# A weight remainder moved from TensorE to VectorE, and a chunk's state update joined with its outputs

## The chip, the cores and the metric

One core of a Trainium2 chip runs the whole program; the other cores are not used. The metric is the time of one execution on the device in microseconds (us). In the rows of the profile PE is TensorE's matmuls, PEld its weight loads, DVE VectorE, ACT ScalarE, POOL GpSimd, and SP SyncE, which issues most of the transfers.

## The reference

A gated linear attention over 768 steps for 4 x 8 heads of size 48, followed by two MLP layers on 3072 tokens of width 384 with 2048 hidden units.

```python
for t in range(S):                         # S = 768, state D x D = 48 x 48 per head, complex
    ar, ai = (a_re_n[:, :, t, :, None], a_im_n[:, :, t, :, None])
    new_re = ar * S_re - ai * S_im
    new_im = ar * S_im + ai * S_re
    kv = np.einsum('bhd,bhe->bhde', k[:, :, t], v[:, :, t])
    S_re, S_im = (new_re + kv, new_im)
    y[:, :, t] = np.einsum('bhd,bhde->bhe', q[:, :, t], S_re)
...
h = x @ w_in                               # first MLP: 384 -> 2048
g = h * np.tanh(softplus(h))
x = g @ w_out                              # 2048 -> 384
...
h = x @ w_in2                              # second MLP
g = h * np.clip(h + 3.0, 0.0, 6.0) / 6.0
out = g @ w_out2
```

Here a_re_n and a_im_n are the decay, scaled to a magnitude under one.

## The kernel before

**Blocks and chunks.** Tokens are worked in 12 blocks of 256 (three for each batch entry); a block is two chunks of 128 steps. For each block `elementwise` (VectorE and ScalarE, lines 589 to 682) forms running products of the decay and multiplies them into q and k. `spread` (L713, twelve transfers issued by SyncE) then lays the results out by head as `rq` and `rk`, and these must be read before the next block's `elementwise` may write `tq` (its first VectorE instruction is L591, behind ScalarE's L590).

**A chunk on TensorE.** `chunk` transposes k (`pk`, evicted by ScalarE as `kt`) and forms the scores (`psc`, L739), which VectorE masks (`am`, L741). `advance` multiplies `kt` with v to the state's update (`pu`, L756), and VectorE carries it into the state `sT`. `second` forms the outputs: `py<-am` (L785) from the masked scores and, except in a sequence's first chunk, `py<-rq,sd` (L791) from the state at the chunk's start, which `turn` transposes (`pst`) and ScalarE evicts as `sd`. The matmuls of `pu` and `py` write 64 rows each; in the profile one such block of eight f32 products is 16 instructions. `pk`, `psc`, `pst`, `pu` and `py` share two PSUM buffers.

**The MLP layers.** Weights and activations are held as two f16 parts, a rounded one (hi) and the remainder (lo), and each product is three matmuls (hi hi, hi lo, lo hi) of 128x256: `ph` (L889) for 384 to 2048, `oa` and `oB` (L902) for 2048 to 384. Between them stand ScalarE's activation, a VectorE multiplication (`s`, L912 or L919), ScalarE's rounding to `gh` (L925) and VectorE's remainder `gl` (L926). `ph` has three PSUM buffers. The layers run as (first MLP, block 0), (first, 1), (second, 0), (first, 2), (second, 1) and so on.

**Weights.** The two weight sets (w1i, w1o for the first MLP, w2i, w2o for the second) come from HBM as 64-bit floats, in 24 pieces of 512 columns for each set. `weights` takes a piece apart: ScalarE converts the low words (L840), VectorE joins the words to an f32 (L841, L842), ScalarE rounds it to the hi part (L843). TensorE then forms the remainder: an f32 matmul of the value with a scaled identity `small` (L845) and an f16 one of the hi part with a negative identity `minus` (L846) add up in a buffer `pw`, which has the tag of `ph`, and ScalarE evicts it as the lo part (L847). The first set is made before the first layer; the second set's pieces are handed out while the first two layers run. Its staging tile `wst` has two buffers and its f32 tile `wt` one.

**The order of the work.** The program is written in one order, and then `arrange` gives each engine another: `survey` lists the instructions with their dependencies and a cost for each, and `plan` schedules them by list, with the costs, in three rounds, and keeps the best. The engines run in exactly that order. Matmuls of 64 rows that `survey` puts into one of its `runs` are scheduled as one piece that stands together; each new run is charged 250 ns more.

Of the kernel before, what the change touches and what calls it, by code (L numbers as in the profile page):

```python
# [10 lines left out]
F32 = mybir.dt.float32  # L11
# [3 lines left out]
AF = mybir.ActivationFunctionType  # L15
ALU = mybir.AluOpType
# [34 lines left out]
SWO = 2.0 ** 5  # L51
# [192 lines left out]
def survey(instructions, first, labels):  # L244
    ENG = mybir.EngineType
    tensor, vector, scalar, pool, sync = ENG.PE, ENG.DVE, ENG.Activation, ENG.Pool, ENG.SP
    after = (tensor, vector, scalar, pool)
    bufs = {"ph": PHB, "oa": 2, "pa": 2, "am": 2, "s1": SPB, "gh": LAG + 1, "gl": LAG + 1, "x2_hi": X2B, "x2_lo": X2B, "wst": 2, "td": 2}
    size = lambda ap: math.prod(n for _, n in ap[1:])

    def adjacent(ap):
        run = 1
        for step, count in list(ap.ap)[:0:-1]:
            if step != run and count > 1:
                break
            run *= count
        return run

    ops, label, tags = [], [], [x[1] for x in labels]
    marks = [x[0] for x in labels] + [1 << 60]  # L260
    j = 0
    for k in range(first, len(instructions)):
        i = instructions[k]
        while marks[j + 1] <= k:
            j += 1
        if i.engine in after or "DMA" in type(i).__name__:
            ops.append(i)
            label.append(tags[j])
    n = len(ops)
    preds = [dict() for _ in range(n)]  # L270
    runs, where, stage = [], {}, {}
    seen, users, rows = {}, {}, {}
    cost, issue, dma, port = [0.0] * n, [0.0] * n, [False] * n, [False] * n
    for k, i in enumerate(ops):
        aps = [(x, False) for x in i.ins if hasattr(x, "bass_ap")] + [(x, True) for x in i.outs if hasattr(x, "bass_ap")]
        tiles = [(x.bass_ap, mybir.dt.size(x.dtype), wr) for x, wr in aps]
        out = tiles[-1][0]
        for ap, width, wr in tiles:
            name = ap.tensor.name
            tag = getattr(ap.tensor, "tag", None)  # L280
            if tag is None:
                continue
            key = tag.split("_")[0] if not tag.startswith("x2_") else tag[:5]
            wr = wr or key in ("oa", "oB")
            whole = key in ("ph", "oa", "oB", "pa", "td")
            box = (0, 128, 0, 1 << 30)
            if not whole:
                p0, lo = divmod(ap.offset, ap.ap[0][0])
                lo += sum(s * (c - 1) for s, c in ap.ap[1:] if s < 0)
                hi = lo + sum(abs(s) * (c - 1) for s, c in ap.ap[1:]) + 1  # L290
                box = (p0, p0 + ap.ap[0][1], lo * width, hi * width)
            if name not in seen:
                seen[name], users[name] = [], []
                row = rows.setdefault(tag, [])
                if row:
                    preds[k][users[row[-1]][0]] = ops[users[row[-1]][0]].engine != i.engine
                row.append(name)
                old = len(row) - 1 - bufs.get(key, 1)
                if old >= 0:
                    for p in users[row[old]]:  # L300
                        preds[k][p] = True
            if users[name]:
                first_use = users[name][0]
                if first_use != k:
                    preds[k].setdefault(first_use, ops[first_use].engine != i.engine)
            users[name].append(k)
            keep = []
            for b, p, pw in seen[name]:
                if (wr or pw) and b[0] < box[1] and box[0] < b[1] and b[2] < box[3] and box[2] < b[3] and p != k:
                    preds[k][p] = preds[k].get(p, False) or pw or ops[p].engine != i.engine  # L310
                if wr and p != k and box[0] <= b[0] and b[1] <= box[1] and box[2] <= b[2] and b[3] <= box[3]:
                    continue
                if not wr and not pw and b == box and tag.startswith("w"):
                    continue
                keep.append((b, p, pw))
            keep.append((box, k, wr))
            seen[name] = keep
        free = max(size(ap.ap) for ap, _, _ in tiles)
        if "DMA" in type(i).__name__:
            dma[k] = True  # L320
            count = math.prod(c for _, c in out.ap)
            issue[k] = 450.0 if out.ap[0][1] > 32 else 625.0
            cost[k] = count * tiles[-1][1] / (360.0 if min(adjacent(ap) * w for ap, w, _ in tiles) >= 2048 else 175.0)
        elif i.engine == tensor:
            passes = 1 if tiles[0][1] == 2 else 2 if i.is_transpose else 4
            cost[k] = passes * size(out.ap) / 2.4 + (2.0 if passes == 1 else 8.0)
            if out.ap[0][1] == 64:
                cost[k] = 115.0
                last = runs[-1][-1] if runs else -1
                if runs and label[last] == label[k] and out.tensor.name == where[last] and stage[last] == tiles[0][0].tensor.tag.split("_")[0]:  # L330
                    runs[-1].append(k)
                else:
                    runs.append([k])
                    cost[k] += 250.0
                where[k], stage[k] = out.tensor.name, tiles[0][0].tensor.tag.split("_")[0]
        elif i.engine == vector:
            fast = type(i).__name__ == "InstMemset" or (type(i).__name__ == "InstTensorScalarPtr" and len(tiles) == 2)
            steps = max(abs(ap.ap[-1][0]) * w for ap, w, _ in tiles)
            cost[k] = 66.0 + free / (1.92 if fast else 0.96) * (1.5 if steps >= 32 else 1.0)
            sb = [ap for ap, _, wr in tiles if not wr and getattr(ap.tensor, "tag", "").split("_")[0] not in ("ph", "oa", "oB", "pa")]  # L340
            port[k] = len(sb) >= 2 or fast
        elif i.engine == scalar:
            psum = tiles[0][0].tensor.tag.split("_")[0] in ("ph", "oa", "oB", "pa")
            cost[k] = (51.0 if psum else 94.0) + 93.0 * sum(size(ap.ap) == 1 for ap, _, _ in tiles) + free / 1.2
        else:
            cost[k] = 46.0 + free * 2.083
            port[k] = True

    return ops, label, preds, cost, issue, dma, port, runs
# [128 lines left out]
def fast_path(ctx, tc, a, out, flag):  # L478
    nc = tc.nc
    mm = nc.tensor.matmul  # L480
    act = nc.scalar.activation
    tt = nc.vector.tensor_tensor
    ts = nc.vector.tensor_scalar
    stt = nc.vector.scalar_tensor_tensor
# [12 lines left out]
    ps_h = ctx.enter_context(tc.tile_pool(name="ps_h", bufs=PHB, space=PSUM))  # L497
# [7 lines left out]
            name=nc.get_next_instruction_name(),  # L505
# [42 lines left out]
    minus = const.tile([128, 2, 128], F16, name="minus")  # L548
    small = const.tile([128, 128], F32, name="small")
# [278 lines left out]
    def weights(idx, nm, s, o):  # L828
        if idx < 2:
            j = next(stage)  # L830
            st = spare(j % 10).bitcast(I32).rearrange("p (n t) -> p n t", t=2)
            t = spare(10 + j % 4 // 2)[:, j % 2 * 1024:][:, :1024].bitcast(I32)
        else:
            st = stp.tile([128, 512, 2], I32, name="wst")
            t = wt.tile([128, 512], I32, name="wt")
        nc.sync.dma_start(out=st, in_=a[nm].bitcast(I32)[:, 2 * o:2 * (o + 512)].rearrange("p (n t) -> p n t", t=2))
        hw, lw = st[:, :, 1], st[:, :, 0]
        tf = t.bitcast(F32)
        hi, lo = W[nm][0][:, o:o + 512], W[nm][1][:, o:o + 512]
        act(out=lw, in_=lw.bitcast(U32), func=AF.Copy, scale=LOW3, bias=-0.5)  # L840
        stt(t, hw, 3, lw, op0=ALU.logical_shift_left, op1=ALU.bitwise_or)  # L841
        stt(t, hw, BUT_SIGN, t, op0=ALU.bitwise_or, op1=ALU.bitwise_and)  # L842
        act(out=hi, in_=tf, func=AF.Copy, scale=s * 2.0 ** -128)  # L843
        pw = ps_h.tile([128, 512], F32, name="pw", tag="ph")
        mm(pw, small, tf, start=True, stop=False)  # L845
        mm(pw, minus[:, idx % 2], hi, start=False, stop=True)  # L846
        act(out=lo, in_=pw, func=AF.Copy, scale=s / SWO)  # L847
        yield

    def weight_guard():  # L850
# [11 lines left out]
    stage = iter(range(24))  # L862
# [116 lines left out]
    start = len(nc.cur_bb.bb.instructions)  # L979
# [133 lines left out]
```

## Time and profile before

| | |
|---|---|
| three executions | 1038.88, 1039.21, 1034.57 us (median 1038.88) |
| the profiled execution | 1037.71 us, span 1035.8 us |
| TensorE busy | 968.7 us, 94% of the span, 8719 matmul instructions |
| VectorE busy | 800.5 us, 77% |
| ScalarE busy | 675.2 us, 65% |
| mean granted clock of TensorE | 0.983 of full speed |

The span runs from the first to the last instruction of the program; the profiled execution's own time has 1.9 us around it. The busy time of an engine is the union of its instructions' times. An instruction's recorded time overlaps with the next one's on TensorE and VectorE, so what one costs in a dense row is read from start to start.

### The profile page before, as it was taken

How to read it: one execution, taken by the hardware profiler on the slowest of the kernel's cores; microseconds unless marked ns; L12 is line 12 of the kernel's file. 1: busy time of each engine (PE TensorE's matmuls, PEld its weight loads, DVE VectorE, ACT ScalarE, POOL GpSimd, SP SyncE). 2: the span in 40 equal slices, each digit the busy share in tenths (PEclk: the TensorE clock that was granted, in tenths of full speed). 3: DMA queues.
4: the chain of work that ended last, by engine and by line, in shares of the span. 5: the costliest groups of instructions: out<-in, count | busy, mean ns of one | idle time of the engine just before them, and what ended most of it. 6: DMA issues, size and time to landing. Idle time of an engine off the chain costs nothing.

```text
span 1035.8 us, 21145 instructions
## 1 busy us (share of the span) xinstructions
PE 968.7 (94%) x8719; PEld 817.9 (79%) x8719; DVE 800.5 (77%) x1455; ACT 675.2 (65%) x1181; POOL 0.9 (0%) x7
## 2 busy tenths in 40 slices
PE   3576889999999999999999999999999999999998
PEld 1144577788888888887888888888887988988887
DVE  7978779979699695895797996895994996654532
ACT  7865789955856846846747747747647747637532
POOL 0000000000000000000000000000000000000000
PEclk9888999999999999999999999999999999999999
DMA  9771854550615126029027146327237227222000
GB/s 357 287 137 45 157 169 143 135 106 24 119 37 100 43 68 112 1 68 166 3 91 158 53 114 151 98 89 156 84 108 131 83 85 155 85 69 77 22 16 19
DMA packets 58681, 106.64 MB, mean 103 GB/s; under 512 B 6482, under 2 KB 40018, under 8 KB 58578
## 3 DMA queue, kind: packets, MB, share of 16 engines
q1 hardware_dynamic: 53586, 100.50, 39.0%
q10 hardware_dynamic: 4992, 4.72, 1.4%
q8 instruction: 70, 1.15, 0.5%
q14 instruction: 33, 0.27, 0.1%
HBM read 80.35 MB, written 4.79 MB: 82 GB/s over the span
## 4 chain that ended last, share of the span: by engine, by line
PE 60%; DVE 16%; ACT 10%; DMA 9%; SPq 2%; issue 2%; ACTq 0%; DVEq 0%
PE ph L889 25%; PE oa L902 16%; PE oB L902 8%; DMA rk<-tq 5%; PE psc L739 3%; PE pw L845 2%; SPq L713 2%; PE py L785 1%; DMA rq<-inp 1%; DVE gl L926 1%; DMA yr<-yr 1%; PE py L791 1%; ACT s L909 1%; DVE s L919 1%; DVE tq L682 1%
## 5 line engine op out<-in xcount | busy, mean ns | idle before, releaser
L926 DVE TENSOR_TENSOR gl<-s,gh 128x512 f16<-128x512 f32 x192 | 131.9, 687 | 53.4 <-ACT gh L925 52.8
L925 ACT ACTIVATE gh<-s 128x512 f16<-128x512 f32 x192 | 120.1, 625 | 76.0 <-DVE s L919 64.2
L889 PE MATMUL ph<-x_hi,w1i_hi 128*128 128x256 f16 x576 | 158.4, 276 | 6.3 <-ACT x_hi L817 3.7
L889 PE MATMUL ph<-x_lo,w1i_hi 128*128 128x256 f16 x576 | 158.6, 276 | 0.2 <-DVE x_lo L818 0.2
L889 PE MATMUL ph<-x_hi,w1i_lo 128*128 128x256 f16 x576 | 158.3, 275 | 0.0
L889 PE MATMUL ph<-x_hi,w2i_hi 128*128 128x256 f16 x576 | 157.1, 273 | 0.0
L889 PE MATMUL ph<-x_hi,w2i_lo 128*128 128x256 f16 x576 | 157.1, 273 | 0.0
L889 PE MATMUL ph<-x_lo,w2i_hi 128*128 128x256 f16 x576 | 157.1, 273 | 0.0
L889 PEld LDWEIGHTS <-w1i_hi 128*128 128x128 f16 x1152 | 113.9, 99 | 23.8 <-issue 8.5
L902 PEld LDWEIGHTS <-w1o_hi 128*128 128x128 f16 x1152 | 113.2, 98 | 20.6 <-issue 6.2
L902 PEld LDWEIGHTS <-w2o_hi 128*128 128x128 f16 x1152 | 112.2, 98 | 16.2 <-issue 4.0
L889 PEld LDWEIGHTS <-w2i_hi 128*128 128x128 f16 x1152 | 111.9, 98 | 14.7 <-issue 2.7
L918 ACT ACTIVATE s<-ph,half 128x512 f32<-128x512 f32 x96 | 65.5, 682 | 80.7 <-PE ph L889 80.6
L902 PE MATMUL oa<-gl,w1o_hi 128*128 128x256 f16 x384 | 105.1, 274 | 4.2 <-DVE gl L926 4.0
L902 PE MATMUL oa<-gh,w1o_hi 128*128 128x256 f16 x384 | 105.2, 274 | 3.2 <-ACT gh L925 3.2
L902 PE MATMUL oa<-gl,w2o_hi 128*128 128x256 f16 x384 | 104.7, 273 | 0.7 <-DVE gl L926 0.7
L902 PE MATMUL oa<-gh,w1o_lo 128*128 128x256 f16 x384 | 105.0, 273 | 0.0
L902 PE MATMUL oa<-gh,w2o_hi 128*128 128x256 f16 x384 | 104.7, 273 | 0.0
L902 PE MATMUL oa<-gh,w2o_lo 128*128 128x256 f16 x384 | 104.7, 273 | 0.0
L919 DVE SCALAR_TENSOR_TENSOR s<-s,ph 128x512 f32<-128x512 f32 x96 | 65.5, 682 | 43.1 <-ACT s L918 42.8
L912 DVE SCALAR_TENSOR_TENSOR s<-s,ph 128x512 f32<-128x512 f32 x96 | 65.6, 684 | 42.6 <-ACT s L911 42.1
L908 ACT ACTIVATE s<-ph 128x512 f32<-128x512 f32 x96 | 56.4, 588 | 24.2 <-PE ph L889 20.8
(153 smaller groups left out, 2076.7 us busy)
## 6 DMA issues: line engine op xcount, KB each, us to landing
wst<-in_w2i_dram SPq DMA_DIRECT2D x24, 512.0 KB
wst<-in_w2o_dram SPq DMA_DIRECT2D x24, 512.0 KB
rq<-inp SPq DMA_DIRECT2D x72, 128.0 KB
rk<-tq SPq DMA_DIRECT2D x72, 128.0 KB
inp<-in_ga_dram SPq DMA_DIRECT2D x11, 768.0 KB
inp<-in_qk_dram SPq DMA_DIRECT2D x11, 768.0 KB
vt<-in_vt_dram SPq DMA_DIRECT2D x24, 256.0 KB
wst<-in_w1i_dram SPq DMA_DIRECT2D x12, 512.0 KB
```

Of the source, the lines that this page charges most:

```text
L682: tt(pl2(tq, 0, 2, 1, w), pl2(pp, 0, 2, 1, w), k_.unsqueeze(1).to_broadcast([128, 2, cols]), op=ALU.mult)
L713: nc.sync.dma_start(out=dst[pl * D + 16 * i:pl * D + 16 * (i + 1), :, :w], in_=vw(src, planes[pl], w)[:, i],)
L739: mm(p[:, hh], rk[:, 4 * g + hh, cs], rq[:, 4 * g + hh, cs], start=True, stop=True)
L845: mm(pw, small, tf, start=True, stop=False)
L889: mm(ph[:, j * w:(j + 1) * w], wt[:, sl], xx[:, k], start=(j == 0 and i == 0), stop=(i == 3 * KD - 1), skip_group_check=True)
L902: mm(po[m], wt[:, sl], gg[:, j * w:(j + 1) * w], start=(ft == 0 and i == 0 and m == 0), stop=(ft == KF - 1 and i == 2), skip_group_check=True)
L908: act(out=s, in_=ph, func=AF.Exp, scale=1.0 / H1)
L912: stt(s, s, 2.5, ph, op0=ALU.subtract, op1=ALU.mult)
L918: act(out=s, in_=ph, func=AF.Relu, scale=1.0 / (6.0 * H2), bias=half)
L919: stt(s, s, 1.0, ph, op0=ALU.min, op1=ALU.mult)
L925: act(out=gh[:, :w], in_=s, func=AF.Copy)
L926: tt(gl[:, :w], s, gh[:, :w], op=ALU.subtract)
```

## The change

Two edits. In `weights` the second set's lo part (idx of 2 and more) is formed by one VectorE instruction, value times scale minus hi part, in place of two matmuls and an eviction; the first set keeps the matmuls. In `survey` a 64-row matmul joins the last run whenever the last instruction of TensorE before it, in the order of writing, was the last of that run; before, it had to have the same label, the same output tile and a first operand of the same tile as well. The pieces of `pu`, `py<-am` and `py<-rq,sd` of one chunk so become one. `general_path` is not touched.

```diff
-    runs, where, stage = [], {}, {}
+    runs, tensor_ops = [], [-2]
...
         elif i.engine == tensor:
+            narrow = out.ap[0][1] == 64
             passes = 1 if tiles[0][1] == 2 else 2 if i.is_transpose else 4
             cost[k] = passes * size(out.ap) / 2.4 + (2.0 if passes == 1 else 8.0)
-            if out.ap[0][1] == 64:
+            if narrow:
                 cost[k] = 115.0
                 last = runs[-1][-1] if runs else -1
-                if runs and label[last] == label[k] and out.tensor.name == where[last] and stage[last] == tiles[0][0].tensor.tag.split("_")[0]:
+                if runs and tensor_ops[-1] == last:
                     runs[-1].append(k)
                 else:
                     runs.append([k])
                     cost[k] += 250.0
-                where[k], stage[k] = out.tensor.name, tiles[0][0].tensor.tag.split("_")[0]
+            tensor_ops.append(k)
...
-        pw = ps_h.tile([128, 512], F32, name="pw", tag="ph")
-        mm(pw, small, tf, start=True, stop=False)
-        mm(pw, minus[:, idx % 2], hi, start=False, stop=True)
-        act(out=lo, in_=pw, func=AF.Copy, scale=s / SWO)
+        if idx < 2:
+            pw = ps_h.tile([128, 512], F32, name="pw", tag="ph")
+            mm(pw, small, tf, start=True, stop=False)
+            mm(pw, minus[:, idx % 2], hi, start=False, stop=True)
+            act(out=lo, in_=pw, func=AF.Copy, scale=s / SWO)
+        else:
+            stt(lo, tf, s * 2.0 ** -128, hi, op0=ALU.mult, op1=ALU.subtract)
```

Since costs and pieces change, `plan` gives every engine a new order. Two places show it. In the changed kernel lines above 270 stand one to four higher (L756 is L757, L785 is L786, L791 is L792, L841 is L842, L842 is L843, L889 is L893, L902 is L906, L912 is L916, L926 is L930).

On TensorE, in a chunk beside the second MLP layer, before:

```order
L889 LDWEIGHTS w2i_lo
L889 MATMUL ph<-x_hi,w2i_lo 128x256
L785 MATMUL py<-am,vt 64x128 x8
L889 LDWEIGHTS w2i_hi
L889 MATMUL ph<-x_hi,w2i_hi 128x256
L889 LDWEIGHTS w2i_hi
L889 MATMUL ph<-x_lo,w2i_hi 128x256
L791 MATMUL py<-rq,sd 64x128 x8
L889 LDWEIGHTS w2i_lo
```

and such a chunk in the changed kernel:

```order
L906 MATMUL oB<-gl,w2o_hi 128x256
L757 MATMUL pu<-kt,vt 64x96 x8
L786 MATMUL py<-am,vt 64x128 x8
L792 MATMUL py<-rq,sd 64x128 x8
L906 LDWEIGHTS w2o_lo
L906 MATMUL oB<-gh,w2o_lo 128x256
```

The chunk's update and its outputs, which had matmuls of the MLP between them, now stand in one piece with the MLP's matmuls ahead of it and behind it.

On VectorE, while the first MLP layer runs and the second weight set is made (`wst` and `wt` are the set's tiles, lines 651 to 666 belong to `elementwise`), before:

```order
L841 SCALAR_TENSOR_TENSOR wt<-wst 128x512
L842 SCALAR_TENSOR_TENSOR wt<-wst,wt 128x512
L651 TENSOR_TENSOR tq<-pp,pre 128x768 x2
L651 TENSOR_TENSOR inp<-pp,pre 128x768
L912 SCALAR_TENSOR_TENSOR s_747<-s_747,ph 128x512
L651 TENSOR_TENSOR inp<-pp,pre 128x768
L660 TENSOR_TENSOR pp<-tq,inp 128x8x6x16
L662 TENSOR_TENSOR pp<-tq,inp 128x8x6x16
L841 SCALAR_TENSOR_TENSOR wt<-wst 128x512
L926 TENSOR_TENSOR gl<-s_707,gh 128x512
L842 SCALAR_TENSOR_TENSOR wt<-wst,wt 128x512
```

and in the changed kernel, where the first MLP layer and the next block's chunk meet:

```order
L843 SCALAR_TENSOR_TENSOR wt<-wst,wt 128x512
L820 TENSOR_REDUCE gm<-x_hi 128x1
L851 SCALAR_TENSOR_TENSOR w2o_lo<-wt,w2o_hi 128x512
L842 SCALAR_TENSOR_TENSOR wt<-wst 128x512
L843 SCALAR_TENSOR_TENSOR wt<-wst,wt 128x512
L916 SCALAR_TENSOR_TENSOR s_964<-s_964,ph 128x512
L930 TENSOR_TENSOR gl<-s_964,gh 128x512
L742 TENSOR_TENSOR am<-psc,cst 128x512 x2
L916 SCALAR_TENSOR_TENSOR s_1027<-s_1027,ph 128x512
L851 SCALAR_TENSOR_TENSOR w2i_lo<-wt,w2i_hi 128x512
L592 TENSOR_TENSOR tq<-tq 128x768
```

Each piece of the set now has a third VectorE instruction, L851, and more of the set's work stands ahead of L592, with which the next block's `elementwise` begins.

## Rows read from the trace of the kernel before

**Rows 1.** The page: busy time by engine; TensorE's busy tenths in 40 slices.

```profile
PE 968.7 (94%) x8719; PEld 817.9 (79%) x8719; DVE 800.5 (77%) x1455; ACT 675.2 (65%) x1181; POOL 0.9 (0%) x7
PE   3576889999999999999999999999999999999998
```

**Rows 2.** The page: the chain that ended last, by engine.

```profile
PE 60%; DVE 16%; ACT 10%; DMA 9%; SPq 2%; issue 2%; ACTq 0%; DVEq 0%
```

**Rows 3.** Windows: length, busy PE PEld DVE ACT POOL, granted clock, DMA share, GB/s.

```profile
150.00:200.00 50.00, 49.13 (x357) 36.20 (x356) 47.70 (x95) 48.95 (x93) 0.00 (x0) 1.00 0.44 132
95.00:290.00 195.00, 182.28 (x1528) 146.07 (x1529) 160.16 (x284) 154.37 (x277) 0.00 (x0) 0.98 0.49 116
290.00:1036.00 746.00, 730.19 (x6943) 644.64 (x6942) 561.04 (x1015) 454.94 (x785) 0.00 (x0) 0.99 0.35 85
```

**Rows 4.** Groups by line and shape: busy us, mean ns, idle before.

```profile
L845 PE MATMUL pw<-wt,small 128*128 128x512 f32 x48 | 27.4, 655 | 4.4 <-DVE s L912 2.9 <-DVE wt L842 1.5
L926 DVE TENSOR_TENSOR gl<-s,gh 128x512 f16<-128x512 f32 x192 | 131.9, 687 | 53.4 <-ACT gh L925 52.8
L842 DVE SCALAR_TENSOR_TENSOR wt<-wst,wt 128x512 int32<-128x512 int32 x24 | 16.5, 688 | 0.3
L912 DVE SCALAR_TENSOR_TENSOR s<-s,ph 128x512 f32<-128x512 f32 x96 | 65.6, 684 | 42.6 <-ACT s L911 42.1
```

**Rows 5.** Timeline of TensorE at 166.7 us: start, duration, instruction.

```profile
166.70 1.02 PE L845 MATMUL pw<-wt,small 128*128 128x512 f32 x2
167.56 0.27 PE L902 MATMUL oa<-gh,w1o_lo 128*128 128x256 f16 x1
167.67 0.38 PE L846 MATMUL pw<-w2i_hi,minus 128*128 128x512 f16 x1
167.88 0.27 PE L902 MATMUL oB<-gh,w1o_hi 128*128 128x256 f16 x1
```

**Rows 6.** Timeline of VectorE at 104.5 us.

```profile
104.49 0.68 DVE L841 SCALAR_TENSOR_TENSOR wt<-wst 128x512 int32<-128x512 int32 x1
105.09 0.69 DVE L926 TENSOR_TENSOR gl<-s,gh 128x512 f16<-128x512 f32 x1
```

**Rows 7.** The chain that ended last, 112 to 138 us.

```profile
122.74 8.02 DMA rk<-tq
```

**Rows 8.** Timeline of TensorE: joined blocks of a chunk, then separate ones.

```profile
136.74 0.88 PE L756 MATMUL pu<-kt,vt 128*64 128x96 f32 x16
...
139.30 0.55 PE L732 MATMUL pk<-cst,rk 96*128 96x96 f32 x4
...
451.68 0.88 PE L756 MATMUL pu<-kt,vt 128*64 128x96 f32 x16
452.50 0.49 PE L739 MATMUL psc<-rq,rk 96*128 96x128 f32 x2
...
454.13 0.27 PE L902 MATMUL oa<-gh,w2o_lo 128*128 128x256 f16 x1
454.33 1.09 PE L785 MATMUL py<-am,vt 128*64 128x128 f32 x16
455.36 0.28 PE L902 MATMUL oB<-gh,w2o_hi 128*128 128x256 f16 x1
```

**Rows 9.** Groups by line, 290 us to the end.

```profile
L785 PE MATMUL py<-am,vt 128*64 128x128 f32 x288 | 19.6, 278 | 0.2 <-ACT sd L800 0.2
L791 PE MATMUL py<-rq,sd 96*64 96x128 f32 x240 | 16.4, 279 | 0.0
L756 PE MATMUL pu<-kt,vt 128*64 128x96 f32 x240 | 13.2, 252 | 0.7 <-DVE am L741 0.7
```

**Rows 10.** A window of 25 us, columns as in rows 3.

```profile
75.00:100.00 25.00, 15.81 (x114) 10.59 (x113) 22.13 (x56) 12.60 (x24) 0.00 (x0) 0.83 0.11 28
```

**Rows 11.** VectorE's waits from 95 to 290 us: us in total, times, longest.

```profile
DVE tq L591 <- ACT tq L590: 9.1, 3, 6.3
DVE gl L926 <- ACT gh L925: 7.3, 8, 2.2
```

## The prediction

> **What bounds the kernel now.** I read the page's busy shares and its 40 slices first [rows 1]: TensorE is busy for 94% of the span, and from the seventh slice on almost without a hole. VectorE has 77%. The chain that ended last agrees: 60% of it is TensorE, 16% VectorE, 10% ScalarE, 9% DMA [rows 2]. Such shares average over stages, so the busy time per stage comes next [rows 3]. Up to 95 us TensorE's slices are half empty: start-up, without an MLP layer. From 95 to 290 us the second weight set is made while the first two MLP layers run, and here TensorE (182.3 of 195 us) and VectorE (160.2) are both close to full; between 150 and 200 us three engines are (49.1, 47.7 and 49.0 of 50). From 290 us on TensorE has 730.2 of 746 us and VectorE 561.0: TensorE alone sets the time.
>
> **What leaves TensorE.** A piece of the second set is two f32 matmul instructions (L845, `pw<-wt,small` x48, so 24 pieces) and one f16 (L846) [rows 4]. Their mean durations overlap with their neighbours', so the price is read from start to start in the timeline: the f32 pair starts at 166.70 and the next matmul at 167.56, 0.86 us; the f16 one starts at 167.67 and the next at 167.88, 0.21 us [rows 5]. Together 1.07 us, and 24 pieces make 25.8 us that leave TensorE's queue. The 24 evictions L847 leave ScalarE, where that makes room between 150 and 200 us.
>
> **What VectorE gets.** 24 SCALAR_TENSOR_TENSORs of 128x512 with an f32 and an f16 operand in SBUF and an f16 result. The trace has none of exactly this form. The nearest rows are L926, the same operand types as a TENSOR_TENSOR, 687 ns, and L842, a SCALAR_TENSOR_TENSOR with two SBUF operands, 688 ns [rows 4]; in a dense stretch such rows start 0.60 us apart (104.49 and 105.09) [rows 6]. I take 0.60 us, 24 of them 14.4 us. Half that, 0.30 us, would be a lower bound (7.2 us), the whole recorded 0.69 us without overlap an upper one (16.5 us); the nearest rows lie at 0.60. Here a rule of the Trainium skill speaks against the change: "Vector Engine (DVE) Microarchitecture Reference", section "7. Points that are easy to get wrong", says that a SCALAR_TENSOR_TENSOR with two non-bf16 SBUF sources halves throughput. By it the additions would be an estimated 24 x 1.2 = 28.8 us, and the sum below would end near 1037 instead of 1022. The row does not show it: L842 is of that form and lasts 688 ns, as long as L912 (684 ns), which has one operand in PSUM [rows 4]. The sum goes by the row.
>
> **The stretch from 95 to 290 us.** Were TensorE its only limit, it would shrink by 25.8 us. VectorE sets a floor before that: 160.2 + 14.4 = 174.6 us of work in a stretch that took 195, so at most 20.4 us can be won with VectorE never idle. It will idle. Where it is fullest now, from 150 to 200 us, it idles 2.3 of 50 us, 4.6% [rows 3]. With that share, 174.6 / 0.954 = 183.0 us: 12.0 us won. The wait most likely to spoil this is the one on the block's spread to heads: `rk<-tq` takes 8.02 us there on the chain that ends last [rows 7], and VectorE stands still for up to 6.3 us before L591, which follows it [rows 11]. The new order puts more of the weight set's VectorE work ahead of that instruction, so I expect most of that hole to be filled. ScalarE is no limit: 154.4 of 195 us [rows 3], and it loses 24 evictions.
>
> **The joined pieces.** In the trace `pu`, `py<-am` and `py<-rq,sd` stand apart. Separate ones: `pu` takes 0.82 us to the next start (451.68 to 452.50), `py` 1.03 us (454.33 to 455.36; the second `py` has the same shape), and the matmul ahead of a block takes 0.20 us to the block's start (454.13 to 454.33), 0.09 more than a plain step (167.56 to 167.67, 0.11 us [rows 5]). Once, at 136.74, the three stand joined: 2.56 us to the next start [rows 8]. With the entries that is 0.82 + 1.03 + 1.03 + 3 x 0.09 = 3.15 us against 2.56 + 0.09 = 2.65: 0.25 us for each of two joins. After 290 us there are 18 chunks (`py<-am` x288, 16 instructions each) with 18 + 15 + 15 = 48 such blocks [rows 9]. The trace has one pair of them joined, so 47 runs; the new order leaves 18. 29 joins x 0.25 = 7.2 us won, where TensorE sets the time. What the few chunks before it save, at most 0.5 us each, VectorE hides.
>
> The join also adds a wait. The state update `pu` now stands right ahead of outputs that need `am` (VectorE) and `sd` (ScalarE), and in TensorE's order the MLP's matmuls queue behind it; behind those, the activations wait. The trace's own waits of this kind after 290 us are 0.7 us (`pu` on `am`) and 0.2 us (`py` on `sd`), once each [rows 9]. So the price lies between nothing and 18 x 0.7 = 12.6 us; since the planner sees these dependencies and puts a piece behind other matmuls, I take 3 us, a quarter of it. The DMA queue of SyncE carries the same transfers; the loads of the second set come a little later beside the same spreads, which I cost at nothing because the two buffers of the staging tile set their pace. If one more spread were held up by them as this one was, it would cost up to the 8.02 us of [rows 7].
>
> **Sum.** Against the profiled execution's own 1037.7 us (span 1035.8 and 1.9 around it; the median of three runs is 1038.9, 1.2 above): 1037.7 - 12.0 - 7.2 + 3.0 = 1021.5, so 1022 us.
>
> **Rivals.** TensorE's full relief: VectorE's additions fit into its holes and the stretch shrinks by 25.8 us: 1037.7 - 25.8 - 7.2 = 1005 us. For it: the order lets the last pieces slip behind the first group of the third layer, so some VectorE work leaves the stretch. Against it: the floor of 174.6 us. Chance 0.12.
>
> The joined piece waits: At 0.7 us in each of the 18 chunks it gives back 12.6 us: 1037.7 - 12.0 - 7.2 + 12.6 = 1031 us. For it: VectorE works in order, and `am` stands behind whatever came first. Against it: 0.9 us of such waits in all of the long stage [rows 9]. Chance 0.13.
>
> TensorE's clock falls: From 75 to 100 us TensorE was busy for 15.8 of 25 us and was granted 0.83, a mixture of the two levels 1.2 and 2.4 GHz [rows 10]; over 95 to 290 us it was granted 0.98 [rows 3]. Without the `pw` matmuls the stretch is thinner: 182.3 - 25.8 = 156.5 us of work. At 0.83 that takes 156.5 x 0.98 / 0.83 = 184.8 us, and with the 12.7 us that it stands idle now 197.5, 2.5 more than before: 1037.7 + 2.5 - 7.2 = 1033 us. The Trainium skill, "TensorE: Matmul & The Clock Gate", section "What's actually happening", says that the throttled state is the default and activity releases it, which would make this so if thinning is enough. Against it: TensorE would still be busy for 156.5 of 183 us, 86%, where the low grant came at 63%. Chance 0.08.
>
> VectorE's waits stay (the other side): If its 34.8 idle us of the stretch (195 - 160.2) are its own, on ScalarE's `tq` and `gh` [rows 11] and not TensorE's doing, the 14.4 us come on top: 1037.7 + 14.4 - 7.2 = 1045 us. For it: 9.1 us of those waits are L591 on L590, behind the spread, and 7.3 us `gl` on `gh`. Against it: `gh` follows `ph`, which TensorE makes earlier now. It decides once more than 20.4 + 7.2 = 27.6 us of idle time remain. Chance 0.10 for that; 0.07 for some 26 us remaining, where 174.6 + 26 = 200.6 us of stretch and 7.2 us won give 1036 us and no change.
>
> **How the numbers follow.** The forecast has 0.50, on its own between 1013 and 1030 us (VectorE's idle share in the stretch between none and 9%, the joins' waits at 3 us). A difference under 0.5%, 5.2 us, is about what a measurement of this kernel can't tell from no change. Faster by more: the forecast, full relief, most of the waiting-piece case, and a part of the clock's, 0.72; within 0.5%: 0.18; slower: 0.10. From 1007 to 1037 us leaves out half of the full-relief case at the bottom and the slower rival at the top, less than 2 in 10.
>
> **What the changed profile would show.** Right: no `pw` on TensorE after the first 95 us; L851 x24 near 0.69 us each; VectorE over 90% busy from 95 us until the set is done, and the work that now stands at 290 us coming 10 to 14 us earlier; `pu`, `py`, `py` in one run of 2.5 us in every chunk; TensorE's idle time after that stretch about 16 us or less, as now. Wrong: L851 at 1.2 us; TensorE waiting on `am` in most chunks; a grant under 0.9 between 95 and 290 us; VectorE under 85% busy there with TensorE idle beside it, which would mean that I took a wait of its own for TensorE's.

## The result, and the profile after

The changed kernel takes 1013.1 us (median of four runs, 1011.3 to 1017.0) where the kernel before took 1037.2 on the same chip (median of four): 24 us less by these medians. The ratio on record is 0.9745, with an interval from 0.971 to 0.978, or some 26 us; it is not the quotient of the two medians, here and in the experiments, and the comparisons below go by it. The forecast was 1022 us. The direction and the places of the gain were right; the stretch and the joins both won more than forecast. The profiled execution took 1011.67 us, with a span of 1009.2.

The page after, its busy times, TensorE's 40 slices and the chain that ended last, beside [rows 1, 2]:

```profile
PE 936.9 (93%) x8647; PEld 813.6 (81%) x8647; DVE 810.0 (80%) x1479; ACT 662.6 (66%) x1157; POOL 0.9 (0%) x7
PE   3577899899989999999999999998999999999998
PE 48%; DVE 18%; ACT 9%; DMA 8%; issue 2%; SPq 1%; ACTq 0%; DVEq 0%
```

TensorE lost 72 matmul instructions and 31.8 us of busy time; VectorE got 24 instructions and 9.5 us, not 14.4. TensorE's idle time grew from 67.1 us to 72.3: it now waits for others a little more. The chain does not show that: it can be followed back only to 132 us here (its shares add up to 86%), so its 48% can't be set beside the 60% of before.

The windows after, with the columns of [rows 3]:

```profile
75.00:100.00 25.00, 17.27 (x107) 13.89 (x108) 24.62 (x62) 10.67 (x22) 0.00 (x0) 0.60 0.26 79
95.00:290.00 195.00, 177.89 (x1623) 154.27 (x1623) 175.27 (x314) 146.39 (x261) 0.00 (x0) 0.95 0.49 114
95.00:237.00 142.00, 127.95 (x1165) 109.88 (x1165) 130.77 (x230) 106.94 (x190) 0.00 (x0) 0.94 0.51 126
```

Until the second set is done, at 237 us, VectorE is busy for 130.8 of 142 us, 92%, and TensorE for 128.0, 90%: two engines now share that stretch about evenly. The granted clock is 0.94 there and 0.95 up to 290 us (0.98 before, [rows 3]), and between 75 and 100 us it fell to 0.60 (0.83 before, [rows 10]).

Groups by line after: the group like that of L842 in [rows 4], and the new instruction.

```profile
L843 DVE SCALAR_TENSOR_TENSOR wt<-wst,wt 128x512 int32<-128x512 int32 x24 | 16.5, 688 | 0.2
L851 DVE SCALAR_TENSOR_TENSOR w2i_lo<-wt,w2i_hi 128x512 f16<-128x512 f32 x12 | 8.2, 686 | 0.8 <-ACT w2i_hi L844 0.7
L851 DVE SCALAR_TENSOR_TENSOR w2o_lo<-wt,w2o_hi 128x512 f16<-128x512 f32 x12 | 8.2, 685 | 0.2 <-ACT w2o_hi L844 0.2
```

L851 lasts 685 ns, as its neighbours do. The halved throughput that the Trainium skill's "Vector Engine (DVE) Microarchitecture Reference", section "7. Points that are easy to get wrong", states for this form is not there.

**A place in the program that both traces have.** VectorE forms 192 activation groups `s` (L912 and L919 before, L916 and L923 after), and the 35th ends near 290 us before. Timeline of VectorE before, the 35th:

```profile
290.47 0.67 DVE L919 SCALAR_TENSOR_TENSOR s<-s,ph 128x512 f32<-128x512 f32 x1
```

and after:

```profile
273.12 0.68 DVE L923 SCALAR_TENSOR_TENSOR s<-s,ph 128x512 f32<-128x512 f32 x1
```

It ends at 291.1 us before and at 273.8 after: 17.3 us were won up to there. From there to the last group it is another 9.1 us. Each such gain is read from one execution of each kernel, and executions of one kernel differ too (the kernel before took 1035.3 to 1047.2 us on one chip). "The early part" and "the long part" below mean the two sides of this instruction.

**Joined pieces.** Timeline of TensorE after, one chunk beside the second MLP:

```profile
436.56 0.88 PE L757 MATMUL pu<-kt,vt 128*64 128x96 f32 x16
437.27 1.04 PE L786 MATMUL py<-am,vt 128*64 128x128 f32 x16
438.14 1.05 PE L792 MATMUL py<-rq,sd 96*64 96x128 f32 x16
439.12 0.28 PE L893 MATMUL ph<-x_hi,w2i_lo 128*128 128x256 f16 x1
```

and the groups of these lines from 290 us to the end, after:

```profile
L786 PE MATMUL py<-am,vt 128*64 128x128 f32 x272 | 17.9, 274 | 0.0
L792 PE MATMUL py<-rq,sd 96*64 96x128 f32 x240 | 15.7, 273 | 0.0
L757 PE MATMUL pu<-kt,vt 128*64 128x96 f32 x224 | 12.3, 252 | 0.0
```

The three stand in one run of 2.56 us (436.56 to 439.12), as forecast, and the idle time before each group is 0.0: no joined piece waited. With the entry, every run of three in the long part took 2.66 us.

### The profile page after: what moved, and what is told of

Read it like the earlier page. It is cut to its first block, busy times and chain, and to the rows that moved or that the text cites. A ratio compares the mean times of both kernels' runs of the same rounds, so it can differ in the third digit from the quotient of the medians.

```text
span 1009.2 us, 20996 instructions
## 1 busy us (share of the span) xinstructions
PE 936.9 (93%) x8647; PEld 813.6 (81%) x8647; DVE 810.0 (80%) x1479; ACT 662.6 (66%) x1157; POOL 0.9 (0%) x7
## 4 chain that ended last, share of the span: by engine, by line
PE 48%; DVE 18%; ACT 9%; DMA 8%; issue 2%; SPq 1%; ACTq 0%; DVEq 0%
PE ph L893 21%; PE oa L906 14%; PE oB L906 7%; DMA rk<-tq 3%; DMA out_dram<-s 2%; DVE gl L930 2%; PE psc L740 2%; DVE s L923 2%; ACT s L913 1%; SPq L714 1%; ACT s L914 1%; ACT s L912 1%; PE py L786 1%; ACT gh L929 1%; PE py L792 1%
## 5 line engine op out<-in xcount | busy, mean ns | idle before, releaser
L930 DVE TENSOR_TENSOR gl<-s,gh 128x512 f16<-128x512 f32 x192 | 131.7, 687 | 50.8 <-ACT gh L929 50.1
L893 PE MATMUL ph<-x_lo,w1i_hi 128*128 128x256 f16 x576 | 158.6, 276 | 3.9 <-DVE x_lo L819 3.9
L893 PE MATMUL ph<-x_hi,w1i_hi 128*128 128x256 f16 x576 | 158.2, 276 | 1.5 <-ACT x_hi L818 0.9
L893 PE MATMUL ph<-x_hi,w2i_hi 128*128 128x256 f16 x576 | 157.6, 274 | 1.7 <-DVE s L916 1.3
L893 PE MATMUL ph<-x_hi,w1i_lo 128*128 128x256 f16 x576 | 158.9, 276 | 0.0
L893 PE MATMUL ph<-x_lo,w2i_hi 128*128 128x256 f16 x576 | 157.6, 274 | 0.0
L893 PE MATMUL ph<-x_hi,w2i_lo 128*128 128x256 f16 x576 | 157.6, 274 | 0.0
L906 PEld LDWEIGHTS <-w1o_hi 128*128 128x128 f16 x1152 | 113.1, 98 | 21.1 <-issue 7.7
L893 PEld LDWEIGHTS <-w1i_hi 128*128 128x128 f16 x1152 | 114.1, 99 | 16.8 <-issue 2.2
L893 PEld LDWEIGHTS <-w2i_hi 128*128 128x128 f16 x1152 | 112.8, 98 | 16.4 <-issue 2.9
L906 PEld LDWEIGHTS <-w2o_hi 128*128 128x128 f16 x1152 | 112.4, 98 | 13.7 <-issue 1.7
L906 PE MATMUL oa<-gl,w1o_hi 128*128 128x256 f16 x384 | 105.2, 274 | 4.9 <-DVE gl L930 4.8
L906 PE MATMUL oa<-gh,w1o_hi 128*128 128x256 f16 x384 | 105.1, 274 | 4.1 <-ACT gh L929 4.1
L906 PE MATMUL oa<-gh,w1o_lo 128*128 128x256 f16 x384 | 105.1, 274 | 0.0
L906 PE MATMUL oa<-gl,w2o_hi 128*128 128x256 f16 x384 | 104.6, 273 | 0.5 <-DVE gl L930 0.5
L916 DVE SCALAR_TENSOR_TENSOR s<-s,ph 128x512 f32<-128x512 f32 x96 | 65.6, 684 | 49.0 <-ACT s L915 48.8
L906 PE MATMUL oa<-gh,w2o_lo 128*128 128x256 f16 x384 | 104.6, 272 | 0.0
L906 PE MATMUL oa<-gh,w2o_hi 128*128 128x256 f16 x384 | 104.6, 272 | 0.0
L923 DVE SCALAR_TENSOR_TENSOR s<-s,ph 128x512 f32<-128x512 f32 x96 | 65.5, 682 | 34.5 <-ACT s L922 34.3
L912 ACT ACTIVATE s<-ph 128x512 f32<-128x512 f32 x96 | 56.4, 588 | 34.5 <-PE ph L893 30.1
## 6 DMA issues: line engine op xcount, KB each, us to landing
rq<-inp SPq DMA_DIRECT2D x72, 128.0 KB
rk<-tq SPq DMA_DIRECT2D x72, 128.0 KB
```

What stands on the lines that cost most here:

```text
L893: mm(ph[:, j * w:(j + 1) * w], wt[:, sl], xx[:, k], start=(j == 0 and i == 0), stop=(i == 3 * KD - 1), skip_group_check=True)
L906: mm(po[m], wt[:, sl], gg[:, j * w:(j + 1) * w], start=(ft == 0 and i == 0 and m == 0), stop=(ft == KF - 1 and i == 2), skip_group_check=True)
L912: act(out=s, in_=ph, func=AF.Exp, scale=1.0 / H1)
L916: stt(s, s, 2.5, ph, op0=ALU.subtract, op1=ALU.mult)
L923: stt(s, s, 1.0, ph, op0=ALU.min, op1=ALU.mult)
L930: tt(gl[:, :w], s, gh[:, :w], op=ALU.subtract)
```

## The experiments

Each time is a median of four or more runs, and each ratio is to the kernel before on the same chip, with its 95% interval. Beside it stands the gain at the 35th group, in the profiled execution against the one before.

**1. The remainder alone**: the change's edit in `weights`, with the `survey` of before.

> The second set's remainder on VectorE, but the pieces of pu and py formed as before the change. Theory (the two edits save in different stages, the first where the second set is made, the second where TensorE alone sets the time): the stretch up to 290 us shrinks by 12 to 15 us as in the changed kernel and the long stage stays near the one of before, 1022 to 1026 us. Rival (the joins save nothing, or only the new order as a whole does): as the changed kernel, 1011 to 1016 us.

1023.9 us, ratio 0.9844 [0.9806, 0.9881]; 19.7 us ahead at the 35th group, and 5.4 of them lost again after it. The total lies in the theory's range, but partly by luck: the early part won more than its 12 to 15 us, and the long part did not stay as it was.

**2. The joined pieces alone**: the change's edit in `survey`, with the `weights` of before.

> Only the joined pieces; the second set's remainder stays on TensorE. Theory: about 33 joins at 0.25 us, nearly all where TensorE alone sets the time, 7 to 8 us, and up to 4 us more if fewer stalls follow: 1026 to 1031 us. Rival (the joined piece waits for the masked scores and the state as long as it saves): 1034 to 1039 us.

1035.2 us, ratio 0.996 [0.9935, 0.9984]; 3.5 us behind at the 35th group, then 6.4 us faster. After 290 us the runs of 64-row matmuls with their entries took 43.2 us for 18 chunks instead of 51.4, so 8.2 us did leave TensorE there. But the total gained about 4 us, which is the rival's range and not the theory's; the early part gave 3.5 us back, and TensorE's idle time in the long part rose from 10.0 us to 13.2, by waits for the activations and for `oB`, not by the joined pieces' own waits for `am` or `sd`.

**3. The remainder twice**:

```diff
+            stt(lo, tf, s * 2.0 ** -128, hi, op0=ALU.mult, op1=ALU.subtract)
             stt(lo, tf, s * 2.0 ** -128, hi, op0=ALU.mult, op1=ALU.subtract)
```

> The changed kernel with L851 issued twice in a row, the second writing the same values again: 14.4 us more for VectorE, nothing for the other engines. Theory (VectorE is now the floor of the stretch in which the second set is made): 10 to 14 us slower than the changed kernel, 1023 to 1027 us. Rival (TensorE still sets that stretch and VectorE has room): at most 3 us slower, 1011 to 1017 us.

1018.5 us, ratio 0.9786 [0.9757, 0.9816]; 9.2 us ahead at the 35th group, 8.1 less than the changed kernel. There the theory's lower end is not quite reached; in the total the loss is 4 to 5 us, between both readings.

**4. The remainder on GpSimd**:

```diff
-            stt(lo, tf, s * 2.0 ** -128, hi, op0=ALU.mult, op1=ALU.subtract)
+            nc.gpsimd.tensor_scalar(tf, tf, s * 2.0 ** -128, None, op0=ALU.mult)
+            ptt(lo, tf, hi, op=ALU.subtract)
```

(`ptt` is GpSimd's `tensor_tensor`.)

> The changed kernel with the remainder formed by GpSimd, which is idle: a scaling of the f32 tile in place and a subtraction, two instructions for each piece in place of L851. Theory (L851's 14.4 us on VectorE are what limits the stretch): VectorE gets them back and TensorE's 25.8 us are won in full, 6 to 11 us faster than the changed kernel, 1002 to 1008 us. Rival (GpSimd's instructions slow VectorE while they run, or the single f32 tile of the set waits for them): 1012 us or more.

1028.7 us, ratio 0.9899 [0.9869, 0.9929], some 15 us behind the changed kernel, in the rival's range, though VectorE has no added work; nothing is won at the 35th group (0.3 us behind). TensorE's longest wait in this kernel, from 95 to 290 us (total, times, longest), was for VectorE's clearing of `oB`:

```profile
PE oB L907 <- DVE oB L977: 13.3, 1, 13.3
```

Timeline of GpSimd in this kernel (L851 and L852 are the two instructions):

```profile
189.99 1.49 POOL L851 TENSOR_SCALAR wt<-wt 128x512 f32<-128x512 f32 x1 [2.34 <-ACT w2o_hi L844]
191.57 1.15 POOL L852 TENSOR_TENSOR w2o_lo<-wt,w2o_hi 128x512 f16<-128x512 f32 x1
196.34 6.48 POOL L851 TENSOR_SCALAR wt<-wt 128x512 f32<-128x512 f32 x1 [3.62 <-ACT w2o_hi L844]
202.91 1.15 POOL L852 TENSOR_TENSOR w2o_lo<-wt,w2o_hi 128x512 f16<-128x512 f32 x1
```

and of VectorE beside the third of them:

```profile
195.58 1.82 DVE L652 TENSOR_TENSOR tq<-pp,pre 128x768 f32<-128x768 f32 x2
197.31 1.83 DVE L652 TENSOR_TENSOR inp<-pp,pre 128x768 f32<-128x768 f32 x2
199.05 0.96 DVE L661 TENSOR_TENSOR pp<-tq,inp 128x768 f32<-128x768 f32 x1
199.92 0.96 DVE L663 TENSOR_TENSOR pp<-tq,inp 128x768 f32<-128x768 f32 x1
200.79 0.69 DVE L931 TENSOR_TENSOR gl<-s,gh 128x512 f16<-128x512 f32 x1
204.09 0.69 DVE L842 SCALAR_TENSOR_TENSOR wt<-wst 128x512 int32<-128x512 int32 x1 [2.62 <-POOL w2o_lo L852]
```

The same GpSimd instruction took 1.49 us, and 6.48 us where VectorE ran two-operand instructions back to back. `wt` has one buffer, so VectorE's next L842 waits for GpSimd, 19.1 us in 14 waits in all, and what is queued behind it on VectorE comes late for TensorE. TensorE's idle time up to the 35th group is 76.0 us, 19.2 more than in the changed kernel. How much of that is GpSimd's doing is not separated: in the longest wait, which ends at 216.5 us, VectorE itself waited for GpSimd only some 2 of the 13.3 us; for the rest it worked on what stands ahead of L977 in this order. An engine that is free by its busy time (GpSimd has 0.9 us of work) did not make the work free.

**5. Half of the remainder**:

```diff
-            stt(lo, tf, s * 2.0 ** -128, hi, op0=ALU.mult, op1=ALU.subtract)
+            stt(lo[:, :256], tf[:, :256], s * 2.0 ** -128, hi[:, :256], op0=ALU.mult, op1=ALU.subtract)
+            nc.gpsimd.memset(lo[:, 256:], 0.0)
```

> The changed kernel, but VectorE forms the remainder of only the left 256 of each 512 columns (24 instructions of about 0.35 us instead of 0.69 us); the right half is set to zero by GpSimd, so the remainder of half of the second weight set is left out. Theory, VectorE is the floor of the stretch from 95 to 290 us: 24 x 0.33 us = 8 us less work there, the end 5 to 8 us earlier than the changed kernel (1005 to 1008 us beside 1013). Rival, the order of the work and the waits of TensorE set the stretch and VectorE has room (as the doubled remainder suggested, which lost only some 4 us): within 3 us of the changed kernel.

1006.3 us, ratio 0.9679 [0.9649, 0.9709]: 7 us less in the median, as the theory said. But its profiled execution is only 1.9 us faster than the changed kernel's, and at the 35th group, behind all of the saved work, it stands 18.2 us ahead of before, beside 17.3. VectorE's busy time up to there is 5.5 us shorter than in the changed kernel and its idle time 4.7 us longer. So where the work was saved it won almost nothing. That speaks against VectorE as the floor at one remainder; at two (experiment 3) it is closer to it. One order stands for each, and the orders of the changed kernel below differ by 4.3 us at this place, so neither is settled. For the total the run is inconclusive, since the next two show that another order alone moves it by more.

**6, 7. Two other orders of the changed kernel's work**: the charge for a run at 0,

```diff
-                    cost[k] += 250.0
```

> The changed kernel with the planner's charge of 250 ns for a run of narrow matmuls set to 0: the same work and the same joined runs (24 of them), planned into another order. A control for what an order alone is worth. Theory, the 26 us come from the work that was taken off TensorE and from the 33 runs that no longer exist: within 5 us of the changed kernel (1008 to 1018 us). Rival, a good part of the gain in the long stage is a lucky order: 5 to 12 us slower (1018 to 1025 us).

and five rounds of `plan` instead of three.

```diff
-ROUNDS = 3
+ROUNDS = 5
```

> The changed kernel planned with five sweeps instead of three, work and joined runs the same: a second control for the order alone. Theory: within 5 us of the changed kernel (1008 to 1018 us). Rival, lucky order: 1018 to 1025 us.

1001.6 us, ratio 0.9638 [0.9611, 0.9664], and 1002.5 us, ratio 0.9643 [0.9615, 0.9672]. Neither expectation held: both are 11 us *faster* than the changed kernel. They have the same instructions and the same 24 joined runs. So the rival was right that an order is worth that much, and wrong in the sign: the changed kernel's order is the slowest of the five tried.

**8. The early chunks planned as before, the other 17 joined**:

```diff
-                if runs and tensor_ops[-1] == last:
+                joint = tensor_ops[-1] == last
+                group += not joint
+                if group <= EARLY:
+                    joint = bool(runs) and label[last] == label[k] and out.tensor.name == where[last] and stage[last] == tiles[0][0].tensor.tag.split("_")[0]
+                if joint:
...
+                where[k], stage[k] = out.tensor.name, tiles[0][0].tensor.tag.split("_")[0]
```

(`EARLY` is 7; the lines that start the counter and the two tables are left out here.)

> The changed kernel in which the first seven chunks keep the pieces of before (the planner may place state update and outputs apart) and the other 17 chunks are one piece each. With the remainder alone the profile stood 18.8 us ahead of before at the 41st activation group, with both edits only 15.4 us. Theory, the early joined pieces cost the difference: 2 to 4 us faster than the changed kernel (1009 to 1011 us). Rival, the 3.4 us are what any other order costs or gives: anywhere within 5 us, with no sign to be foretold.

1011.1 us, ratio 0.9726 [0.9693, 0.9759], the same as the changed kernel within the intervals. It settles little: the planner placed only one of the early chunks apart (25 runs instead of 24), so it is one more order, 2.4 us better at the 35th group and 1.9 us worse after it.

**9 to 12. Other orders of the parts.** Five rounds for the kernel before and for the remainder alone, charge 0 for the joined pieces alone, and both for the changed kernel.

> The kernel before, planned with five sweeps instead of three: work and runs of narrow matmuls (57) the same, another order. What an order alone is worth without the change. Two orders of the changed kernel gave 1001.6 and 1002.5 us, 11 us under the changed kernel itself. Theory, orders of the same work scatter by some 5 us to either side: 1030 to 1046 us. Rival, more sweeps find a better order for any kernel, and the gain of five sweeps is a thing of its own: 1024 to 1031 us, 8 to 14 us faster than before.

> The change's remainder alone (pieces planned as before), with five sweeps. The remainder alone with three sweeps took 1023.9 us. Theory (scatter): 1016 to 1030 us, and the mean of both orders 14 to 20 us under that of the kernel before. Rival (five sweeps help everywhere): 1010 to 1016 us.

> The joined pieces alone (the remainder on TensorE), with the charge for a run set to 0: the same 24 runs as the joined pieces alone, which took 1035.2 us beside 1040.2 of before, in another order. Five sweeps give here the same order as three, so the charge was changed instead. Theory (the runs saved some 8 us in the profile and the order of the early stretch gave part of it back): 1026 to 1036 us. Rival, joined pieces are worth less than 5 us whatever the order: 1034 to 1042 us.

> Both edits with the charge at 0 and five sweeps: a fifth order of the changed kernel's work, tried for a faster version. Theory (scatter): 1000 to 1014 us. Rival (charge 0 and five sweeps each help and add up): 990 to 997 us.

The kernel before came out in its theory's range. The remainder alone with five rounds came out in the rival's (five sweeps help everywhere), and so speaks against scatter alone. The joined pieces with charge 0 were faster than either reading had it, and the last one is 0.4 us faster than its theory's range and short of its rival's.

All orders, with the gains of the profiled execution on either side of the 35th group:

| | us | ratio to before | early part | long part |
|---|---|---|---|---|
| before, five rounds | 1036.5 | 0.9971 [0.9946, 0.9996] | 1.0 | -4.2 |
| remainder alone | 1023.9 | 0.9844 | 19.7 | -5.4 |
| the same, five rounds | 1013.9 | 0.9745 [0.9684, 0.9806] | 21.3 | 3.2 |
| joined alone | 1035.2 | 0.996 | -3.5 | 6.4 |
| the same, charge 0 | 1021.2 | 0.9796 [0.9743, 0.9848] | 0.5 | 14.0 |
| the change | 1013.1 | 0.9745 | 17.3 | 9.1 |
| the same, charge 0 | 1001.6 | 0.9638 | 17.3 | 18.0 |
| the same, five rounds | 1002.5 | 0.9643 | 21.6 | 12.6 |
| the same, early chunks apart | 1011.1 | 0.9726 | 19.7 | 7.2 |
| the same, charge 0, five rounds | 999.6 | 0.9589 [0.9542, 0.9636] | 18.0 | 19.5 |

Orders of the same work lie from 0.3% (before) to 1.6% (joined alone, and both edits) apart. The two settings are no neutral draws: in every pair of rows five rounds were faster than three (0.3%, 1.0%, 1.0%, 0.5%), and charge 0 was faster than 250 ns (1.6%, 1.1%, 0.5%). So a setting can be a gain of its own; the kernel before and the remainder alone were not run at charge 0, which leaves that open. An edit is therefore priced between rows of the same settings. The remainder is worth 1.6% over the kernel before, 2.3% over it at five rounds, and on top of the joined pieces 2.2%, or 1.6% at charge 0: 16 to 24 us. The joined pieces are worth 0.4% over the kernel before, and on top of the remainder 1.0%, at three rounds as at five: 4 to 11 us. Both together are worth 26 us at the settings of the change and 34 at five rounds. Each such price carries the intervals of two ratios, 3 to 6 us to either side each, and one order on either side, so the joined pieces' price is not known closer than that. The last row, the best of the five orders of both edits, is the fastest kernel found, 1.6% under the changed one by the ratios.

The last row's page, busy times:

```profile
PE 933.4 (93%) x8647; PEld 811.6 (81%) x8647; DVE 810.9 (81%) x1479; ACT 663.6 (66%) x1157; POOL 0.9 (0%) x7
```

Its instructions are those of the changed kernel, and TensorE's busy time is only 3.5 us less; the rest is waiting that is gone. TensorE's waits from 290 us to the end, in this kernel:

```profile
PE oB L905 <- DVE oB L975: 1.4, 2, 1.1
PE oa L905 <- DVE gl L929: 1.0, 3, 0.4
```

and in the changed one:

```profile
PE oB L906 <- DVE oB L976: 3.4, 2, 2.5
PE oa L906 <- ACT gh L929: 1.9, 2, 1.3
PE oa L906 <- DVE gl L930: 1.4, 4, 0.6
PE psc L740 <- ACT kt L734: 0.6, 2, 0.4
```

## Why the prediction was right, and where its terms were off

The work that moves, its price on either engine and the two places of the gain were read rightly, and so the time fell, by more than forecast. That 1013.1 us lies inside the range from 1007 to 1037 us is in part luck: three of the five orders of the same work took 999.6 to 1002.5 us, below that range.

**What leaves TensorE: 25.8 us: right.** With the remainder alone TensorE's busy time fell from 968.7 [rows 1] to 944.2 us in one order and 941.6 in the other, by 24.5 and 27.1. No `pw` stands after the first 95 us.

**The price of one L851: right, 685 ns**; the rival price of 1.2 us is out.

**The stretch: 12.0 us forecast, 17.3 measured in the changed kernel, 17.3 to 21.6 over its five orders.** The mis-sized term is "174.6 us of work" over a busy share of 95.4%. VectorE's idle time up to the 35th group fell from 50.6 to 25.3 us, by 25.3; the forecast implied 12.0 + 14.4 = 26.4, so the holes were filled as I expected. But VectorE's busy time up to there rose by 7.9 us, not by 14.4. From the trace: the 24 instructions add 16.5 us of recorded time; other work up to there is 3.2 us less (mostly three instructions of `elementwise`, 2.9 us, that slipped behind the group); and 5.3 us more of the recorded time overlaps, since VectorE's work fell into 78 unbroken stretches instead of 116. With 20 more instructions and 38 fewer stretches, 58 more instructions follow another without a hole, and 58 x 0.09 us (0.69 recorded, 0.60 in a row) is 5.2 us. I charged 0.60 to the new instructions and kept the old ones as they stood in the holes. Experiment 5 suggests more: half the added work on VectorE won only 0.9 us more there, so a floor of VectorE's may not be what ended the stretch at all. The "full relief" of 25.8 us was not reached either: TensorE's busy time up to the 35th group fell by 22.1 us and its idle time grew by 4.7.

**The joins: 7.2 us won and 3.0 us given back in the forecast; about 8 us won and nothing given back by waits of the pieces.** The 8.2 us of experiment 2 for 29 joins are 0.28 us each (0.25 forecast). The wait term fell: `am` and `sd` were always there. In the long part the seven joined orders of the table won 6.4 to 19.5 us, 12.4 in the mean, and the three others -5.4 to 3.2. So more can be won than the runs hold; the sum had kept TensorE's other waits and its clock as they were. They make up the rest. Take the runs' 8.2 us (where joined), add TensorE's idle time that is gone and half of its work at the low clock that is gone (last section): this comes within some 2 us of the long part's gain in every row of the table. In the changed kernel it is 8.2 us, less 0.5 (10.5 us idle instead of 10.0), plus 1.7 (3.4 us at the low clock instead of 6.8), 9.4 against 9.1 measured. With charge 0 it is 8.2 + 4.8 + 3.4 = 16.4 against 18.0, and for the remainder alone 0 - 5.4 + 0 = -5.4 against -5.4. Why the planner's order leaves fewer waits in one row than in another stays open.

**The clock: a part of the rival came true.** The grant from 95 to 290 us fell from 0.98 [rows 3] to 0.95, though TensorE was still 91% busy, and the stretch won all the same. The Trainium skill, "TensorE: Matmul & The Clock Gate", section "What's actually happening", describes a throttled default that activity releases, and the windows in the last section agree. Up to the 35th group TensorE did 31.3 us of its work at the low level, a grant of 0.50, where before it did 20.9. Work at that level takes twice as long (matmuls of 128x256 start 0.21 us apart at 489 us of the kernel before, and 0.11 apart at 491.2), so half of the added 10.4 us, 5.2 us, is lost by an estimate from these. The sum had no such term. With the 4.7 us of added idle time that makes 9.9 us, beside the 8.5 that the early part lacks of the full relief (25.8 - 17.3).

**The rival that VectorE's waits stay: it did not come true.** Of the 9.1 us that L591 waited [rows 11], 1.6 are left after, and `gl` on `gh` has 3.0 instead of 7.3. VectorE's waits after, from 95 to 290 us:

```profile
DVE am L742 <- PE psc L740: 4.6, 4, 1.9
DVE s L923 <- ACT s L922: 3.9, 1, 3.9
DVE gl L930 <- ACT gh L929: 3.0, 1, 3.0
DVE tq L592 <- ACT tq L591: 1.6, 1, 1.6
```

The longest are now on TensorE and ScalarE, each a few us: no wait of one kind is left that more room on VectorE would remove, which fits experiment 5.

**TensorE's idle time after the stretch: right**, 15.4 us from the 35th group to the end (about 16 forecast), 14.9 before; up to the last group it is 10.5 and 10.0.

**What the sum did not have** is the order itself as a term: it put every microsecond down to an edit, while the same edits in five orders lie between 999.6 and 1013.1 us. The forecast's 15.7 us fall short of the 26 of the result, and of the 34 that both edits are worth at five rounds.

## What to carry to other kernels

Where a list scheduler sets the order, any edit redraws the whole order, and one order is one sample: plan the same work two or three ways, before and after, and compare rows of the same planner settings before a gain of 1% is put down to an edit. When work is moved to a half-idle engine, cost the holes that it fills as well: what ran behind another instruction was cheaper here than what stood alone (0.60 us instead of 0.69), so the busy time grew by less than the sum of the additions. And read a free engine's price from its own instructions beside its neighbours', not from its idle time.

## What the runs showed of the hardware that was not expected

**A standstill of TensorE costs twice.** The kernel before, in windows of one to three us (columns as in [rows 3]):

```profile
485.00:487.00 2.00, 0.33 (x3) 0.16 (x3) 2.00 (x2) 2.00 (x6) 0.00 (x0) 1.00 0.88 227
487.00:488.00 1.00, 0.61 (x4) 0.47 (x4) 0.95 (x3) 1.00 (x3) 0.00 (x0) 0.77 1.01 356
488.00:490.00 2.00, 2.00 (x11) 1.39 (x10) 1.44 (x3) 1.65 (x4) 0.00 (x0) 0.50 0.96 343
490.00:491.00 1.00, 1.00 (x7) 0.74 (x5) 0.69 (x1) 0.97 (x3) 0.00 (x0) 0.53 0.77 271
```

TensorE did 0.33 us of work from 485 to 487 us; when it went on, the clock was granted at 0.50 (1.2 GHz) until shortly before 491, some 3.4 us in which half of the work is lost: 1.7 us on top of the 2 us of waiting. The kernel before has a second such place, after waits from 788 us on:

```profile
792.00:794.00 2.00, 2.00 (x11) 1.39 (x10) 1.27 (x2) 1.82 (x4) 0.00 (x0) 0.50 0.59 212
```

Together that is 6.8 us at the low clock in its long part, and 3.4 us lost. The long part of the changed kernel, which starts at 273.8 us, has one such place, at 278 us:

```profile
278.00:281.00 3.00, 0.16 (x2) 0.00 (x0) 0.69 (x1) 1.42 (x2) 0.00 (x0) 1.00 1.13 159
281.00:282.00 1.00, 0.77 (x7) 0.80 (x8) 0.00 (x0) 0.80 (x2) 0.00 (x0) 0.80 1.07 347
282.00:285.00 3.00, 3.00 (x17) 2.65 (x16) 1.56 (x2) 2.97 (x6) 0.00 (x0) 0.50 0.40 138
```

So one wait of 2 or 3 us can weigh more than its own length. Not each does: in the changed kernel TensorE stands still for 2.5 us at 689.5 us, and the clock stays at 1.00 behind it:

```profile
688.00:692.00 4.00, 1.53 (x15) 1.23 (x13) 0.27 (x1) 2.64 (x5) 0.00 (x0) 1.00 1.13 150
692.00:694.00 2.00, 1.98 (x19) 1.77 (x19) 0.69 (x1) 1.94 (x5) 0.00 (x0) 1.00 1.12 369
```

What decides between the two is not shown here.

**GpSimd beside VectorE.** An instruction of 1.5 us grew to 6.5 us while VectorE ran two-operand f32 instructions without a gap (experiment 4); the Trainium skill, "GPSIMD Engine Reference", section "1. Specifications", states that it shares its SBUF interfaces with VectorE and contends with VectorE's instructions of two SBUF inputs. The trace agrees, and shows the size here.

**A VectorE instruction of half the columns is not half the price:** 421 ns for 256 columns against 685 ns for 512.
